# A new token order, block transposes for the first two batches and 32x32 score tiles in an attention kernel with two MoE layers

## The chip, the cores and the metric

The kernel runs on one core of one Trainium2 chip. The metric is the device time of one execution in microseconds (us). Of the kernel before, three runs took 1302.26, 1302.63 and 1302.87 us.

## The reference, cut to what matters

```python
def sm_attn(qq, kk, vv):                       # 8 batches, 8 heads, 576 tokens, head width 64
    s = scale * np.matmul(qq, kk.transpose(0, 1, 3, 2))
    a = np.exp(s - np.max(s, axis=-1, keepdims=True))
    a = a / (np.sum(a, axis=-1, keepdims=True) + 1e-09)
    return np.matmul(a, vv)
p_packed = sm_attn(p, k, v)                    # 32 packed queries a head read all tokens
x = sm_attn(q, p_packed, p_packed)             # all tokens read the 32 packed rows
...                                            # x to [4608, 512]
h = x @ w_in; x = (h - np.tanh(h)) @ w_out     # first layer, width 2048
...                                            # second layer: each token to one expert of 8, width 1024
out[mask] = gate_w[mask, None] * (np.maximum(x[mask] @ w1[e], 0.0) @ w2[e])
```

The order in which the 4608 tokens are kept on the chip is free, as long as every row of the output is written to its place.

## The kernel before, in words

**Slots.** The two layers are one row of slots, and the loop at the end of the kernel (L1047) goes through them. A slot of the first layer is a half batch (288 tokens) and one block of 128 hidden columns: `gemm1` (L719), the function h - tanh(h) in four ScalarE and four VectorE instructions (`chain`, L730), three slots later `gemm2` (L764). There are 256: slots 0 to 31 are batch 0 in plain float32, slots 32 to 255 the other batches with every operand split into a high and a low part (three products each, `mm3`, L95). The input of `gemm1` is not v: w_in is multiplied by the packed rows first (`m_pe`, L210), so that a slot multiplies softmax weights `a` by `m`. Then come 144 slots of the second layer.

**Ahead of slot 0** stand 31 more slots (-31 to -1, `NPRO` and `LEAD`) with the attention of batch 0 and the first of the weight conversions. The first of them puts the loads on the SyncE queue.

**Attention** (`attention`, L246) of batch b is hung on slots: `post` entries are loads and VectorE work, `stage(t, fn, *evs)` puts TensorE work `fn` on slot base + t and what reads its result on the next slot. All of it goes through one PSUM tile, `AT` (two banks, L68), so each stage waits until the one ahead is read out. Its steps: k transposed (head width on the partitions), scores of the packed queries (`scores1`), maximum, exponential and sum (`s1max`, `s1exp`, `s1sum`), the weights transposed (`a1t_pe`), times v (`p1_pe`), that transposed (`ppt_pe`), scores of q against the packed rows (`scores2`), softmax over 32 (`sm2a` to `sm2d`).

Two forms exist. For batches 0 and 1 (`by_pe`) k and q are loaded in 1536-byte runs and transposed on TensorE against an identity (`flip_pe`, eight calls a batch, twelve matmuls each) and copied out of `AT` (`flip_ev`). For batches 2 to 7 the loads put 32 elements (128 bytes) to a run, 32 loads a batch for k and q, and VectorE transposes 32x32 blocks (`prep`, L317, eight instructions a batch).

**Weight conversions.** w_in and w_out come as float64; 32 steps (`conv_a`, L158) turn a 512 KB piece into float32: two VectorE instructions (L161, L165), three on ScalarE (L169 to L171), one on GpSimd (L177). Four buffers take the pieces (`raw_load`, L136), loaded two steps ahead; the steps lie on slots -21 to 16. The sixteen w_out pieces are split afterwards (`conv_b`, L186).

**Batch b > 1** starts at slot 32(b-1) + 5, batch 1 at slot 0; its `m_pe` from slot 21 of its stretch of 32 on. The order inside a slot is the program's; between engines a scheduler moves instructions past each other.

Of the kernel before, what the change touches and what calls it, by code (L numbers as in the profile page):

```python
# [2 lines left out]

# [18 lines left out]
EPS = 1e-9  # L22
# [3 lines left out]
def attn_moe_moe_kernel(  # L26
# [26 lines left out]
    LAG = 3  # L53
    NWH = NF
# [54 lines left out]
    def consts2(sp):  # L109
        wg = sp.tile([128, 4, NE], F32, name="wg")  # L110
        nc.sync.dma_start(out=wg, in_=w_gate.rearrange("(c p) e -> p c e", p=128))
        md = evp.tile([32, B, 18, 2], I32, name="md", tag="rt_b")
        nc.sync.dma_start(
            out=md, in_=mod_id.bitcast(I32).rearrange("(b i k two) -> i b k two", b=B, i=32, two=2)
# [12 lines left out]
        nc.vector.tensor_copy(out=modi.rearrange("i (b k) -> i b k", b=B), in_=md[:, :, :, 0])  # L127
# [30 lines left out]
    def conv_a(key):  # L158
# [51 lines left out]
    def m_pe(b, u):  # L210
        def rhs(g, hh):
# [5 lines left out]
            lambda g, hh: AT[32 * hh:32 * hh + 32, g, 0:256],  # L217
# [4 lines left out]
    def m_ev(b, u):  # L222
        ps = AT[:, :, 0:256]
# [22 lines left out]
    def attention(ap, b):  # L246
        r = {}

        def nat_tile(shape):
            return ap.tile(shape, F32, name="nat", tag="nat", bufs=2)  # L250

        by_pe = b < 2

        def load_pair(src, nm, j):
            if by_pe:

                t = r[nm, j] = nat_tile([96, 2, 2, 6 * D])
                for g in range(2):
                    h0 = 4 * g + 2 * j
                    nc.sync.dma_start(  # L260
                        out=t[:, g], in_=src[b, h0:h0 + 2].rearrange("h (a c) d -> a h (c d)", c=6)
                    )
                return

            t = nat_tile([128, 2, 18, 32])
            for g in range(2):
                for e in range(2):
                    q0 = 64 * g + 32 * e
                    for x in range(2):
# [643 lines left out]
    with ExitStack():  # L913
# [34 lines left out]
        def place(grp, base):  # L948
# [4 lines left out]
            for t, fn in pe.items():  # L953
                at_pe(base + t, fn)
# [169 lines left out]
```

## Time and profile before

| | us |
|---|---|
| median of the three runs | 1302.63 |
| the profiled execution, its own time | 1304.62 |
| its span | 1302.9 |
| start of slot 0 (first `gemm1`) | 64.94 |
| start of slot 32 | 206.66 |
| first matmul of the second layer | 881.8 |

The span runs from the first to the last instruction of the profile; what lies around it makes the execution's own time. A stage is the stretch between two of these starts. "Busy" of an engine is the sum of its instructions in a stretch; a matmul of float32 is two rows in the trace, so `x16` is eight of them.

### The profile page before, as it was taken

The page shows a single profiled execution, that of the slowest core. Times are in us where ns is not written, and L with a number is a line of the kernel's source. Part 1 is how long each engine was busy: PE and PEld are TensorE (multiplying, and loading weights), DVE is VectorE, ACT ScalarE, POOL GpSimd, SP SyncE. Part 2 cuts the span into 40 slices and gives each one's busy share as a digit, 9 for nine tenths or more (in the row PEclk, how much of TensorE's full clock was granted, in tenths as well). Part 3 has the DMA queues.
Part 4 walks back from the last instruction along what each step waited for, and adds up shares of the span by engine and source line. Part 5 has one row for each costly group of instructions (what it writes and reads, how often), then busy time and mean ns, then how long its engine had stood idle before and what let it go on. Part 6 is the DMA issues. An engine that isn't in the chain of part 4 may idle for free.

```text
span 1302.9 us, 26482 instructions
## 1 busy us (share of the span) xinstructions
PE 1225.3 (94%) x10018; PEld 1070.6 (82%) x10019; DVE 828.0 (64%) x1931; ACT 718.4 (55%) x1848; POOL 166.7 (13%) x174
## 2 busy tenths in 40 slices
PE   4597889999999999999999999999999999999996
PEld 3365568978988988978988978989999999999995
DVE  2577699798898798898898897895212121111211
ACT  3589877777767767767777777772111111111111
POOL 1123220110111110110111112250000000000000
PEclk9998899999999999999999999999999999999998
DMA  6757535435345245245245024332221221222201
GB/s 173 199 172 203 144 90 165 101 106 146 69 114 139 64 121 147 49 123 143 48 126 144 20 96 144 95 102 69 63 84 56 67 74 64 82 65 82 66 17 35
DMA packets 192533, 132.40 MB, mean 102 GB/s; under 512 B 123280, under 2 KB 171408, under 8 KB 192400
## 3 DMA queue, kind: packets, MB, share of 16 engines
q1 hardware_dynamic: 192400, 130.65, 36.4%
q8 instruction: 80, 1.31, 0.4%
q14 instruction: 53, 0.43, 0.1%
HBM read 98.10 MB, written 32.51 MB: 100 GB/s over the span
## 4 chain that ended last, share of the span: by engine, by line
PE 70%; DVE 16%; ACT 5%; issue 4%; DMA 2%; POOL 1%; SPq 1%; DVEq 0%; ACTq 0%; POOLq 0%
PE acc L97 12%; PE acc L99 11%; PE acc L98 11%; PE h L97 9%; PE h L98 8%; PE h L99 8%; DVE gs L748 2%; DVE gs L750 2%; PE at L201 2%; PE at L294 2%; DVE th L744 2%; DVE gl L761 2%; PE acc L770 1%; DVE qq L746 1%; PE at L342 1%
## 5 line engine op out<-in xcount | busy, mean ns | idle before, releaser
L97 PE MATMUL acc<-gh,wo_hi 128*128 128x288 f32 x960 | 293.8, 308 | 6.0 <-ACT gh L759 5.1
L99 PE MATMUL acc<-gl,wo_hi 128*128 128x288 f32 x960 | 276.8, 298 | 6.3 <-DVE gl L761 3.4
L98 PE MATMUL acc<-gh,wo_lo 128*128 128x288 f32 x960 | 281.5, 295 | 0.0
L97 PEld LDWEIGHTS acc<-gh,wo_hi 128*128 128x128 f32 x960 | 179.9, 188 | 41.0 <-ACT u L740 11.4
L99 PEld LDWEIGHTS acc<-gl,wo_hi 128*128 128x128 f32 x960 | 177.1, 188 | 14.2 <-DVE gl L761 6.9
L98 PEld LDWEIGHTS acc<-gh,wo_lo 128*128 128x128 f32 x960 | 180.3, 188 | 0.7 <-issue 0.4
L99 PE MATMUL h<-xbl,w1h 128*128 128x256 f32 x576 | 162.3, 282 | 0.0
L98 PE MATMUL h<-xbh,w1l 128*128 128x256 f32 x576 | 162.1, 281 | 0.0
L97 PE MATMUL h<-xbh,w1h 128*128 128x256 f32 x576 | 161.5, 280 | 0.0
L761 POOL TENSOR_TENSOR gl<-gs,gh 128x288 fp32r<-128x288 f32 x105 | 85.6, 816 | 575.6 <-ACT gh L759 424.9
L744 DVE TENSOR_TENSOR th<-h,th 128x288 f32<-128x288 f32 x256 | 114.8, 448 | 54.9 <-ACT mk L742 51.5
L750 DVE COPY_PREDICATED gs<-mk,th 128x288 f32<-128x288 int32 x256 | 139.3, 544 | 2.8
L97 PE MATMUL h<-ah,mh 128*128 128x288 f32 x448 | 135.2, 302 | 5.7 <-DVE gs L748 5.7
L740 ACT ACTIVATE u<-h 128x288 f32<-128x288 f32 x256 | 106.4, 416 | 56.7 <-PE h L99 40.3
L862 DVE SCALAR_TENSOR_TENSOR bl<-h,bh 128x256 fp32r<-128x256 f32 x72 | 30.6, 425 | 164.0 <-ACT bh L861 163.9
L98 PE MATMUL h<-ah,ml 128*128 128x288 f32 x448 | 132.2, 295 | 0.0
L743 ACT ACTIVATE qq<-u 128x288 f32<-128x288 f32 x256 | 114.8, 449 | 30.9 <-DVE gs L748 25.0
L99 PE MATMUL h<-al,mh 128*128 128x288 f32 x448 | 131.8, 294 | 0.0
L746 DVE SCALAR_TENSOR_TENSOR qq<-qq,u 128x288 f32<-128x288 f32 x256 | 121.6, 475 | 13.4 <-ACT qq L743 10.5
L759 ACT ACTIVATE gh<-gs 128x288 fp32r<-128x288 f32 x240 | 108.0, 450 | 36.6 <-PE acc L98 35.3
L741 ACT ACTIVATE th<-h 128x288 f32<-128x288 f32 x256 | 105.0, 410 | 34.2 <-DVE gs L750 32.0
L861 ACT ACTIVATE bh<-h 128x256 fp32r<-128x256 f32 x72 | 27.6, 384 | 171.4 <-PE h L99 169.8
(145 smaller groups left out, 2462.3 us busy)
## 6 DMA issues: line engine op xcount, KB each, us to landing
ws<-w_in_v SPq DMA_DIRECT2D x56, 512.0 KB
nat<-in_v_dram SPq DMA_DIRECT2D x16, 576.0 KB
x_hi<-x2h SPq DMA_DIRECT2D x16, 576.0 KB
x_lo<-x2l SPq DMA_DIRECT2D x16, 576.0 KB
xbh<-x_hi SPq DMA_DIRECT2D x18, 512.0 KB
xbl<-x_lo SPq DMA_DIRECT2D x18, 512.0 KB
raw<-in_moe_w_in_dram SPq DMA_DIRECT2D x32, 256.0 KB
raw<-in_moe_w_out_dram SPq DMA_DIRECT2D x16, 512.0 KB
```

The source lines that it names most:

```text
L97: nc.tensor.matmul(out=ps, lhsT=ah, rhs=bh, start=first, stop=False)
L98: nc.tensor.matmul(out=ps, lhsT=al, rhs=bh, start=False, stop=False)
L99: nc.tensor.matmul(out=ps, lhsT=ah, rhs=bl, start=False, stop=last)
L740: nc.scalar.activation(out=u, in_=ps, func=ACTF.Square)
L741: nc.scalar.activation(out=th, in_=ps, func=ACTF.Tanh)
L743: nc.scalar.activation(out=qq, in_=u, func=ACTF.Exp, scale=-PK)
L744: nc.vector.tensor_tensor(out=th, in0=ps, in1=th, op=ALU.subtract)
L746: nc.vector.scalar_tensor_tensor(out=qq, in0=qq, scalar=PB, in1=u, op0=ALU.add, op1=ALU.mult)
L750: nc.vector.copy_predicated(gs, mk, th)
L759: nc.scalar.activation(out=gh, in_=gs, func=ACTF.Copy)
L761: eng.tensor_tensor(out=gl, in0=gs, in1=f32(gh), op=ALU.subtract)
L862: nc.vector.scalar_tensor_tensor(out=gl, in0=ps, scalar=0.0, in1=f32(gh), op0=ALU.max, op1=ALU.subtract)
```

## The change

**Token order.** Token t of a batch is 288a + 9i + c (a half of two, i of 32, c of 9; before 18i + 9a + c). With a and i on 64 partitions, nine tokens of a head lie behind each other: one load of k, q or v is 64 partitions x 2 heads x 2304 bytes. All batches use this form, 12 loads a batch, and v is loaded like k and q. Output rows and the modality ids follow the order.

**Transposes.** `flip_pe` and `flip_ev` are gone. `prep` transposes 32x32 blocks on VectorE, for all batches, which leaves token i on the free axis and 32 of the 64 head columns (index e) on the partitions of half a. So the products over the head width are now sums of two matmuls with 32 rows.

**Score tiles.** `scores1(g)` has 16 matmuls of 32 rows x 32 columns (before 8 of 64 x 32) and `scores2(half)` 16 (before 8). `s1exp` is one instruction of 576 elements (before two of 288). `a1t_pe` is 18 matmuls against the identity in tiles of 64 columns (before 12 transposes of 96 columns). `p1_pe` is 72 matmuls of 64 rows (before 48 of 96). `ppt_pe` has eight more matmuls, and `ppt_ev` one more copy (`ppS`).

**Start.** Batch 0's attention is no longer on slots: it is a list, written out, with six PSUM banks instead of two (`AT` and two tiles in the banks that `gemm2` takes later). Eight of the 32 conversion steps and two of the eight `m_pe` lie in that list; eight steps lie on slots 0 to 7, the rest on 8 to 20; pieces are loaded three steps ahead. Batch 1's attention starts at slot 9 (before 0), its `m_pe` at slot 25 (before 21).

```diff
-            if by_pe:
-
-                t = r[nm, j] = nat_tile([96, 2, 2, 6 * D])
...
-            t = nat_tile([128, 2, 18, 32])
...
+            t = r[nm, j] = ap.tile([128, 2, 9 * D], F32, name="nat", tag="nat", bufs=NAT)
+            for g in range(2):
+                h0 = 4 * g + 2 * j
+                nc.sync.dma_start(
+                    out=t[64 * g:64 * g + 64], in_=src[b, h0:h0 + 2].rearrange("h (a c) d -> a h (c d)", c=9)
+                )
...
+        def scores1(g):
+            ps = ps_of("s1", g)
+            for e in range(2):
+                for a in range(2):
+                    rows = slice(64 * g + 32 * a, 64 * g + 32 * a + 32)
+                    for hh in range(4):
+                        nc.tensor.matmul(
+                            out=ps[32 * hh:32 * hh + 32, a, 0:HW],
+                            lhsT=r["pT"][rows, hh, e, :],
+                            rhs=r["kT", hh // 2][rows, hh % 2, :, e, :],
+                            start=(e == 0), stop=(e == 1), tile_position=(64 * g + 32 * a, 32 * hh),
+                        )
...
-            av = r["a1", g].rearrange("p c i m -> p c (i m)")
-            for c in range(6):
-                nc.tensor.transpose(AT[0:96, c // 3, 128 * (c % 3):128 * (c % 3) + 128], av[:, c], ident)
...
+        def a1t_pe(n):
+            ps = ps_of("a1t", n)
+            for c in range(6 * n, min(6 * n + 6, 9)):
                 for g in range(2):
...
+                        lhsT=r["a1", g][:, c].rearrange("p a i -> p (a i)"), rhs=ident,
                         start=True, stop=True, tile_position=(0, 64 * g),
...
+        def p1_pe():
+            ps = ps_of("p1", 0)
+            for c in range(9):
                 for hh in range(4):
...
+                    for g in range(2):
+                        rows = slice(64 * g, 64 * g + 64)
                         nc.tensor.matmul(
...
+                            start=(c == 0), stop=(c == 8), tile_position=(64 * g, 32 * hh),
                         )
...
         def ppt_pe():
...
+            for e in range(2):
+                for q0 in range(0, 128, 32):
+                    nc.tensor.matmul(
+                        out=ps[q0:q0 + 32, 0, 128 + 128 * e:256 + 128 * e],
+                        lhsT=r["pps"][:, q0 // 64, 32 * e:32 * e + 32], rhs=ident,
+                        start=True, stop=True, tile_position=(0, q0),
+                    )
...
         def scores2(half):
...
+            ps = ps_of("s2", half)
+            for e in range(2):
+                for hh in range(4):
+                    for g in range(2):
+                        q0 = 64 * g + 32 * half
+                        nc.tensor.matmul(
+                            out=ps[32 * hh:32 * hh + 32, g, 0:HW],
+                            lhsT=r["ppS"][q0:q0 + 32, e, hh, :],
+                            rhs=r["qT", hh // 2][q0:q0 + 32, hh % 2, :, e, :],
+                            start=(e == 0), stop=(e == 1), tile_position=(q0, 32 * hh),
+                        )
...
+        A.load_pair(k, "k", 0)
+        A.load_p()
+        A.load_pair(k, "k", 1)
+        A.load_pair(q, "q", 0)
+        raw_load(ck[0])
+        raw_load(ck[1])
+        consts()
+        run(A.prep_p, lambda: A.prep("k", 0))
+        A.load_pair(v, "v", 0)
+        run(lambda: A.prep("k", 1))
+        A.load_pair(v, "v", 1)
+        A.scores1(0)
+        A.scores1(1)
+        run(lambda: A.prep("q", 0))
...
+        run(lambda: A.s1max(0), lambda: A.s1exp(0), lambda: A.s1max(1), lambda: A.s1exp(1))
+        A.a1t_pe(0)
+        run(lambda: A.s1sum(0), lambda: A.s1sum(1), lambda: conv_step(0))
+        A.a1t_ev(0)
+        A.a1t_pe(1)
+        run(lambda: conv_step(1))
...
+        A.scores2(0)
+        A.scores2(1)
+        m_pe(0, 0, X[1])
+        run(lambda: conv_step(3), lambda: A.sm2a(0), lambda: A.sm2b(0), lambda: m_ev(0, 0, X[1]))
...
-            place(attention(ap, b), 2 * NF * (b - 1) + (0 if b == 1 else 5))
+            place(attention(ap, b, lambda *key: AT).stages(), 2 * NF * (b - 1) + (9 if b == 1 else 5))
```

TensorE, from the first instruction to the first `gemm1`, before (`at` is the PSUM tile, L294 the flips, L725 `gemm1`):

```order
L294 MATMUL at<-ident,nat 64x96 x48
L342 MATMUL at<-T,pT 32x288 x16
L294 MATMUL at<-ident,nat 64x96 x48
L385 MATMUL at<-ident,a_210 96x128 x6
L385 MATMUL at<-ident,a_240 96x128 x6
L396 MATMUL at<-nat,a1T 32x64 x48
L414 MATMUL at<-ident,pps 64x128 x2
L201 MATMUL at<-T,ppT 32x288 x8
L201 MATMUL at<-wv,ppT 32x256 x8
L201 MATMUL at<-T,ppT 32x288 x8
L201 MATMUL at<-wv,ppT 32x256 x16
L725 MATMUL h<-a2w,m_w 128x288 x2
```

The same place in the changed kernel, from `p1_pe` on (L352; `x_105` and `x_106` are the two further PSUM tiles, L396 `scores2`, L203 `m_pe`, L673 `gemm1`):

```order
L352 MATMUL x_105<-nat,a1T 32x64 x72
L371 MATMUL x_106<-ident,pps 64x128 x2
L377 MATMUL x_106<-ident,pps 32x128 x8
L396 MATMUL at<-T,ppS 32x288 x16
L396 MATMUL x_105<-T,ppS 32x288 x16
L203 MATMUL x_106<-wv,ppT 32x256 x8
L203 MATMUL at<-wv,ppT 32x256 x8
L673 MATMUL h<-a2w,m_w 128x288 x5
```

The 96 flips are gone, and the stages that stood behind each other in `at` now lie in three tiles. Two `m_pe` stand ahead of the first `gemm1`, before three.

VectorE in the changed kernel, in the softmax of the first half of batch 0, from the maximum (L412) to the transpose that `gemm1` waits for (L438); L163 and L167 are conversion steps:

```order
L412 TENSOR_REDUCE m_401<-s_398 128x18
L414 TENSOR_TENSOR s_398<-s_398,m_401 128x576
L163 TENSOR_SCALAR raw_219<-raw_219 128x512
L167 SCALAR_TENSOR_TENSOR raw_219<-raw_219 128x512
L427 TENSOR_REDUCE m_427<-s_398 128x18
L163 TENSOR_SCALAR raw_237<-raw_237 128x512
L429 TENSOR_SCALAR m_427<-m_427 128x18
L167 SCALAR_TENSOR_TENSOR raw_237<-raw_237 128x512
L431 RECIPROCAL m_427<-m_427 128x18
L433 TENSOR_TENSOR s_398<-s_398,m_427 128x576
L163 TENSOR_SCALAR raw_335<-raw_335 128x512
L438 STREAM_TRANSPOSE a2w<-s_398 128x576
```

Three conversion steps, the fourth to sixth of the 32, stand in that chain with five of their six instructions. The second half's softmax comes behind it; before, its first instructions stood between those of the first half.

## Rows read from the trace of the kernel before

**Rows 1.** The page: span, and busy time, share and instructions of each engine over the whole span.

```profile
span 1302.9 us, 26482 instructions
PE 1225.3 (94%) x10018; PEld 1070.6 (82%) x10019; DVE 828.0 (64%) x1931; ACT 718.4 (55%) x1848; POOL 166.7 (13%) x174
```

**Rows 2.** Busy time by stage: stretch in us, its length, then busy us of each engine (instructions in brackets), the granted clock of TensorE, the mean share of the DMA engines and GB/s. The stretches are: ahead of slot 0; slots 0 to 16; slots 17 to 31; slots 32 to 255; the second layer.

```profile
0.00:64.94 64.94, 34.60 (x417) 22.79 (x418) 24.58 (x64) 28.68 (x57) 10.09 (x16) 1.00 0.72 185
64.94:154.37 89.43, 75.96 (x573) 53.32 (x573) 65.06 (x135) 76.69 (x169) 26.76 (x23) 0.90 0.68 190
154.37:206.66 52.29, 48.06 (x378) 36.10 (x377) 50.77 (x115) 40.27 (x107) 8.15 (x8) 1.00 0.37 109
206.66:881.80 675.14, 656.29 (x6019) 585.87 (x6018) 599.55 (x1414) 501.25 (x1347) 119.30 (x125) 1.00 0.40 105
881.80:1302.90 421.10, 410.37 (x2639) 372.50 (x2638) 88.09 (x206) 71.48 (x173) 2.43 (x3) 0.99 0.20 64
```

**Rows 3.** TensorE's waits ahead of slot 0 (0 to 64.9 us): for whom, us in total, how often, the longest.

```profile
PE at L294 <- ACT T L305: 5.3, 3, 3.8
PE at L294 <- DMA nat<-in_k_dram: 4.6, 2, 4.2
PE at L294 <- DVE T L313: 4.4, 3, 1.5
PE at L201 <- DVE s L436: 3.2, 2, 2.0
```

**Rows 4.** Groups of instructions ahead of slot 0 (0 to 64.94 us): line, engine, operation, out<-in, shapes, count, busy us and mean ns of one, idle time before them.

```profile
L294 PE MATMUL at<-ident,nat 96*64 96x96 f32 x192 | 18.0, 372 | 16.8 <-ACT T L305 5.3 <-DMA nat<-in_k_dram 4.6 <-DVE T L313 4.4
L165 DVE SCALAR_TENSOR_TENSOR raw<-raw 128x512 int32<-128x512 int32 x10 | 6.9, 687 | 0.3
L169 ACT ACTIVATE raw<-raw 128x512 int32<-128x512 f32 x9 | 6.0, 668 | 6.7 <-DVE raw L165 6.6
L161 DVE TENSOR_SCALAR raw<-raw 128x512 int32<-128x512 int32 x10 | 4.7, 468 | 11.8 <-DMA raw<-in_moe_w_in_dram 11.8
L396 PE MATMUL at<-nat,a1T 96*32 96x64 f32 x96 | 2.8, 311 | 0.9 <-ACT a1T L389 0.9
L369 ACT ACTIVATE a<-at,nm 128x288 f32<-128x288 f32 x4 | 2.0, 497 | 5.3 <-DVE nm L356 5.3
L389 ACT ACTIVATE a1T<-at 96x768 f32<-96x768 f32 x2 | 1.6, 807 | 2.9 <-PE at L385 2.9
L351 DVE TENSOR_REDUCE mx<-at 128x2 f32<-128x576 f32 x2 | 1.5, 758 | 9.8 <-PE at L342 9.8
L414 PE MATMUL at<-ident,pps 128*64 128x128 f32 x4 | 0.7, 445 | 0.6 <-ACT pps L408 0.6
```

**Rows 5.** The timeline at some places of the first 66 us: start, us, engine, line, what, count, idle time before it and what ended it.

```profile
4.17 0.55 PE L294 MATMUL at<-ident,nat 96*64 96x96 f32 x2 [4.17 <-DMA nat<-in_k_dram]
19.99 2.15 PE L342 MATMUL at<-T,pT 64*32 64x288 f32 x16 [0.75 <-ACT T L305]
55.28 0.85 DVE L436 STREAM_TRANSPOSE s<-at 128x288 f32<-128x288 f32 x2 [3.17 <-PE at L201]
64.12 0.77 DVE L467 STREAM_TRANSPOSE a2w<-s 128x576 f32<-128x576 f32 x1
64.94 2.29 PE L725 MATMUL h<-a2w,m_w 128*128 128x288 f32 x4 [0.49 <-DVE a2w L467]
```

**Rows 6.** Slots 0 to 31 (64.94 to 206.66 us): groups as in Rows 4, then TensorE's longest wait in that stretch.

```profile
L169 ACT ACTIVATE raw<-raw 128x512 int32<-128x512 f32 x23 | 15.8, 688 | 4.8 <-DVE raw L165 3.6 <-POOL wv L177 0.6
L294 PE MATMUL at<-ident,nat 96*64 96x96 f32 x192 | 12.4, 293 | 3.4 <-ACT m_w L226 2.1 <-DVE T L313 1.2
L315 ACT ACTIVATE T<-at 128x288 f32<-128x288 f32 x4 | 2.7, 686 | 1.0 <-PE at L294 1.0
L313 DVE COPY T<-at 128x288 f32<-128x288 f32 x4 | 2.7, 674 | 1.0 <-ACT T L315 1.0
L305 ACT ACTIVATE T<-at 128x576 f32<-128x576 f32 x4 | 2.6, 648 | 0.8 <-PE at L294 0.8
PE h L725 <- DVE gs L748: 8.0, 4, 3.9
```

**Rows 7.** TensorE in batch 4's attention (timeline, columns as in Rows 5): `scores1`, one `a1t_pe`, `p1_pe`, `ppt_pe`, one `scores2`.

```profile
417.91 1.17 PE L342 MATMUL at<-T,pT 64*32 64x288 f32 x16
429.98 0.82 PE L385 MATMUL at<-ident,a 128*96 128x128 f32 x6
440.93 1.55 PE L396 MATMUL at<-nat,a1T 96*32 96x64 f32 x96
448.42 0.44 PE L414 MATMUL at<-ident,pps 128*64 128x128 f32 x4
453.75 0.71 PE L201 MATMUL at<-T,ppT 64*32 64x288 f32 x16
```

**Rows 8.** TensorE's largest waits in slots 32 to 255 (206.66 to 881.8 us).

```profile
PE h L97 <- DVE gs L748: 5.7, 11, 1.3
PE acc L97 <- ACT gh L759: 3.1, 6, 0.5
PE at L201 <- DVE rt_t L555: 3.1, 6, 0.5
```

**Rows 9.** VectorE's 32x32 block transposes of k and q over the whole span, columns as in Rows 4.

```profile
L320 DVE STREAM_TRANSPOSE T<-nat 128x576 f32<-128x576 f32 x48 | 36.8, 766 | 0.0
```

More of the change, by code (lines that the diff above doesn't have):

```diff
@@ L2 @@
 from inspect import isgenerator
+from types import SimpleNamespace
 import concourse.bass as bass
@@ L333, in scores1 @@
         def scores1(g):
-            rows = slice(64 * g, 64 * g + 64)
-            for half in range(2):
-                for hh in range(4):
-                    kk = r["kT", hh // 2][rows, hh % 2]
-                    if by_pe:
-                        kk = kk[:, 9 * half:9 * half + 9, :].rearrange("p r i -> p (r i)")
-                    else:
-                        kk = kk.rearrange("p (m c) i -> p m c i", m=3)[:, :, 3 * half:3 * half + 3, :]
-                    nc.tensor.matmul(
-                        out=AT[32 * hh:32 * hh + 32, half, 0:HW],
-                        lhsT=r["pT"][rows, hh, :],
-                        rhs=kk,
-                        start=True, stop=True, tile_position=(64 * g, 32 * hh),
-                    )
+            ps = ps_of("s1", g)
@@ L705, in other_half @@
                 )
-            rows = out[bass.ds(b * S, S), :].rearrange("(i r) d -> r i d", r=18)[9 * half + 3 * t:9 * half + 3 * t + 3]
+            rows = out[bass.ds(b * S + half * HW, HW), :].rearrange("(i c) d -> c i d", c=9)[3 * t:3 * t + 3]
             o = ox.tile([96, 512], F32, name="oo")
@@ L977, in at_cv @@
             cv_ev.setdefault(n, []).append(fn)
-        NPRO = 24
-        LEAD = 7
-        place(attention(ap, 0), -NPRO)
+        NPC = 8
+        cslot = {}
+        for i in range(len(ck) + 1):
+            if i < NPC:
+                m = -1
+            elif i < 2 * NPC:
+                m = i - NPC
+            else:
+                m = 8 + (i - 2 * NPC) * 3 // 4
+            if m >= 0:
+                at_cv(m, lambda i=i: conv_step(i))
+            if i < len(ck):
+                cslot[ck[i]] = m
@@ new lines, in attn_moe_moe_kernel, with run @@
+        for f in range(NWH // 2):
+            at_cv(NWH + 1 + f * 11 // 7, lambda f=f: conv_b((1, f)))
+        def run(*fns):
+            for _ in seq(fns):
+                pass
+        ps0 = tc.alloc_tile_pool(name="ps0", bufs=1, space=PSUM)
+        X = [ps0.tile([128, 2, 512], F32, name=f"x{c}") for c in range(2)]
+        PS0 = {
+            ("s1", 0): AT, ("s1", 1): X[0], ("a1t", 0): X[1], ("a1t", 1): AT, ("p1", 0): X[0], ("ppt", 0): X[1],
+            ("s2", 0): AT, ("s2", 1): X[0],
+        }
@@ L1046, in attn_moe_moe_kernel @@
         total = len(slots)
-        for n in range(-NPRO - LEAD, total + LAG + 2):
-            if n == NF + 1:
+        for n in range(total + LAG + 2):
+            if n == NF + 5:
                 early.release()
```

328 lines of the change are left out of this document (128 added, 200 removed).

## The prediction

> **What bounds the kernel now.** I read the busy shares first, then the busy time by stage, then the waits and the single rows of each stage. TensorE is busy 94% of the span [rows 1], but the stages differ [rows 2]. In the second layer (881.8 us on) it has 410 of 421 us of work; the change leaves that stage alone. In slots 32 to 255 it has 656 of 675 us; VectorE has 600. Ahead of slot 0 no engine is the bound: TensorE is busy 34.6 of 64.9 us, ScalarE 28.7, VectorE 24.6. There the reader is to see a chain: flips wait for ScalarE's copies, for VectorE's copies and for k [rows 3], because everything goes through one PSUM tile. In slots 0 to 31 (141.7 us) three engines share the load: TensorE 124.0 us, ScalarE 117.0, VectorE 115.8 (two rows of that view added) [rows 2].
>
> So there are three places to look at: how much earlier slot 0 starts, whether slots 0 to 31 keep their length, and what the longer attention costs where TensorE is full.
>
> **The start.** Slot 0 starts at 64.94 and waits last for the transposed softmax of half 0 [rows 5]. I follow the new list from row to row. The first flip got its first k load at 4.17 [rows 5]. The queue now holds k and p (1.3 MB by shape) before anything else; at the 185 GB/s of this stretch [rows 2] that is 7.1 us, so k is there at 8 (estimate; 7 to 10). Two block transposes of 0.77 [rows 9]: 9.6. `scores1(0)`, 2.15 at the durations of this stretch [rows 5]: 11.8. The maximum, then two block transposes of q that stand ahead of the negation, the other maximum, small steps: 0.76 + 1.53 + 0.76 + 0.5 [rows 4, 9]: 15.3. Two exponentials, each less than two of 0.50 and more than one, say 0.9 [rows 4]: 17.1. On ScalarE five of the first six conversion instructions stand ahead of the copy of the transposed weights, 5 x 0.67 and 0.81 [rows 4]: 21.2; TensorE's transposes run beside that. `p1_pe`, 2.8 before [rows 4], now nine rounds for twelve but 144 rows for 96, so 2.1 to 4.2, and it waits for the second copy: 25. Two copies, `ppt_pe` (0.7 and two more rounds), two more copies [rows 4]: 28.5. `scores2(0)`, now two rounds, 2.15: 30.7. The softmax of half 0 took 9.6 from its first transpose to the end of its last, 55.28 to 64.89 [rows 5], with conversion steps and half 1 between its instructions; now other conversion steps stand there and half 1 doesn't, so 9: 39.7. The sixth conversion piece, which VectorE reads ahead of the last transpose, is the 6.8th MB of the queue: 37 us at 185 GB/s, 26 if the engines, busy at 0.72 [rows 2], were filled. That hides behind the chain, just. Slot 0 at 39.5: **-25.4 us** (35 to 46: -30 to -19).
>
> **Slots 0 to 31.** What moves in or out, by engine. TensorE loses batch 1's flips, 12.4 us [rows 6], and gains about 2.5 (one `m_pe` more, the longer attention below): 114. ScalarE had run nine conversions' first instruction before slot 0 [rows 4], now five: 4 x 3 x 0.67 = +8.0; it loses eight copies, 2.7 + 2.6 [rows 6], and about 1.0 of exponentials: 119. VectorE had begun ten, now six: 4 x (0.47 + 0.69) = +4.6 [rows 4]; it gains eight block transposes, +6.1 [rows 9], loses four copies, -2.7 [rows 6], and gains the part of half 1's softmax that now falls behind slot 0, about 2.4: 126. The sum over the three is 357 before and 359 now, only shifted from TensorE to VectorE. So I keep the length and add a little, because VectorE was already busy 50.8 of 52.3 us in slots 17 to 31 [rows 2] and four conversions now end there: **+3 us** (-9 to +11).
>
> **Slots 32 to 255**, six batches of attention, all on a full TensorE. `scores1` took 1.17 for two rounds of 288 columns, `scores2` 0.71 for one [rows 7], so a round is 0.46 (1.6 ns a column) and starting a group 0.25. `scores1` keeps two rounds: 0. `scores2` gets a second: 2 x 0.46 = +0.92. `a1t_pe`: nine rounds of 128 columns, 1.84, with two starts 2.34, for 2 x 0.82 [rows 7]: +0.70. `ppt_pe`: two rounds of 128: +0.41. `p1_pe`: twelve rounds in 1.30 and a start before [rows 7], now nine: -0.32; if it is the 16 ns an instruction (1.55 / 96) that set its time, 144 of them make 2.3: +0.78. The Trainium skill, "TensorE: Matmul & The Clock Gate", part 1, has a rule that speaks against many small matmuls: starts are never closer than some 25 ns, by which `p1_pe` would be 3.6 us, +2.1, and the kernel, by an estimate from that page, near 1298. The trace disagrees with it: 96 rows in 1.55 us are 16 ns apart [rows 7]. No row shows tiles of 32 rows; I take eight at a time, as the 64-row tiles of `scores2` ran, and keep four at a time as the other end (a rival below). Sum +1.7 a batch (to 2.8), +10 in six (to 17). Against it stands TensorE's idle time here, 18.9 us [rows 2]; the named waits are for VectorE and ScalarE being late [rows 8], mostly behind `scores2`. The new matmuls stand ahead of them, so VectorE gets that time and part of the waits closes; I give back 6. ScalarE's shorter exponentials and the larger DMA runs are costed at nothing: none of these waits is for a DMA, and ScalarE is busy only 501 of 675. Net **+4 us** (-2 to +17).
>
> **Sum.** -25.4 + 3 + 4 = -18.4. The profiled execution took 1304.62, 2.0 above the median 1302.63, so 1286.2 in its terms and **1284** as a median.
>
> **Rivals.**
> *The gain is given back in slots 0 to 31.* VectorE at 126 us is the fullest engine, slots 17 to 31 were full of it, and four conversions with three splits (some 7 us) go there; pieces must also come at 190 GB/s or more, with the engines at 0.68 [rows 2]. TensorE waited 8.0 us for VectorE here [rows 6], and its granted clock was 0.90 in slots 0 to 16 [rows 2], part of that stretch at the lower of 1.2 and 2.4 GHz; more waiting could bring more of it. For it: these rows. Against: the total load does not grow. Price +10 over the forecast: 1294.
> *`p1_pe` and its like are bound by instructions.* At the 16 ns of rows 7, `p1_pe` costs +0.78 and not -0.32, and the same rate on the other added rows adds about as much again in the six batches with nothing left to absorb it: +6, 1290. The rule of the Trainium skill weighed above, in "TensorE: Matmul & The Clock Gate", lies beyond this case in the same direction.
> *Slower: tiles of 32 rows run four at a time.* Place: `scores1`, `scores2`, `p1_pe` in the six full batches. `scores1` and `scores2` go to four rounds: 2 x 0.92 + 2 x 1.38; `p1_pe` to 18 rounds of 0.108: +0.64; with +0.70 and +0.41 that is 6.35 a batch, 38 in six, of which the idle time takes 12 at most: +26. At the start two calls double, and `p1_pe`: +6; batch 1: +5. Net -25.4 + 3 + 6 + 5 + 26 = +15: 1317. It decides from about 4.5 us more a batch. For it: no row has such tiles. Against: two groups of 64 rows ran together (0.71 for 16 matmul rows against 1.17 with one group) [rows 7]. The Trainium skill, "TensorEngine Tiling (Array Packing)", Key Properties, says that tiles work independently, and lists 16 of them for 32x32; that speaks for eight at a time, and the trace agrees for tiles of 64 rows.
> *Better.* Slot 0 at 36, slots 0 to 31 shorter by 8 since TensorE waits less for one PSUM tile, the waits of rows 8 gone: 1270.
>
> **Numbers.** Forecast 0.56; given back 0.18; instructions 0.10; better 0.08; slower 0.08. Range 1269 to 1299: below it half of the better case, above it the slower case and a quarter of the given-back one. A difference under 0.2% (2.6 us) can't be told from no change. Faster: the forecast, instructions, better and 0.11 of the given-back case, 0.85; the same: 0.06 of that case; slower: 0.01 of it and the slower case, 0.09.
>
> **What would show it.** First `gemm1` at 36 to 43 us; first high/low product of slot 32 at 178 to 194; slots 32 to 255 in 673 to 685 us; `scores2` near 1.2 us for 32 matmul rows, `scores1` too, `a1t_pe` 2.3 in both, `p1_pe` 1.2. VectorE and not TensorE the fullest engine in slots 0 to 31. Wrong if `scores1` takes near 2.1 us, if slot 0 starts after 46, or if slots 0 to 31 take more than 155 us.

## The result, and the profile after

The changed kernel took **1312.26 us** (median; four runs, 1311.21 to 1313.25), the kernel before 1302.45 in the runs beside it: 1.008 of it, 95% interval 1.0062 to 1.0099. It is slower by 0.8%; the forecast was 1284. The profiled execution took 1311.34, 6.7 more than the profiled one of before (1304.62); the shares of the stages below are shares of these 6.7, not of the 9.8 between the medians.

The page of the changed kernel: span, then busy us, share and instructions of each engine.

```profile
span 1309.6 us, 27913 instructions
PE 1232.9 (94%) x10850; PEld 1064.0 (81%) x10851; DVE 840.4 (64%) x1939; ACT 705.7 (54%) x1808; POOL 167.5 (13%) x174
```

Busy time by stage, columns as in [rows 2]: ahead of slot 0; slots 0 to 31; slots 32 to 255; second layer.

```profile
0.00:42.00 42.00, 19.44 (x361) 10.95 (x362) 20.81 (x52) 14.97 (x29) 6.80 (x12) 0.85 0.75 188
42.00:195.60 153.60, 126.60 (x910) 82.72 (x909) 125.98 (x269) 122.14 (x279) 38.16 (x36) 0.91 0.62 173
195.60:888.90 693.30, 676.49 (x6947) 597.76 (x6946) 605.48 (x1415) 497.34 (x1330) 120.07 (x125) 1.00 0.35 104
888.90:1309.60 420.70, 410.40 (x2640) 372.53 (x2638) 88.12 (x206) 71.27 (x173) 2.45 (x3) 0.99 0.21 64
```

Against [rows 2] the start is 22.9 us shorter (forecast 25.4), slots 0 to 31 are 11.9 longer (forecast 3), slots 32 to 255 18.2 longer (forecast 4), and the second layer is 0.4 shorter: +6.7 in the span. The start came within its range. Both other stages failed.

**Slots 0 to 31.** The same view in three pieces, slots 0 to 15, 16 to 23, 24 to 31; the changed kernel first, the kernel before second.

```profile
42.00:112.44 70.44, 58.15 (x294) 34.84 (x293) 59.83 (x125) 56.12 (x127) 18.18 (x17) 0.94 0.76 209
112.44:164.36 51.92, 41.72 (x424) 27.34 (x423) 36.06 (x74) 44.13 (x98) 13.98 (x13) 0.84 0.60 161
164.36:195.62 31.26, 26.76 (x197) 20.56 (x195) 30.11 (x72) 21.91 (x55) 5.99 (x6) 0.95 0.36 109
```

```profile
64.94:146.48 81.54, 68.85 (x540) 49.05 (x540) 60.53 (x128) 71.14 (x156) 25.71 (x22) 0.93 0.68 194
146.48:179.99 33.51, 30.23 (x216) 20.82 (x217) 29.40 (x64) 25.83 (x66) 4.08 (x4) 0.91 0.42 101
179.99:206.66 26.67, 24.93 (x194) 19.55 (x193) 25.90 (x60) 20.00 (x53) 5.11 (x5) 1.00 0.39 128
```

Slots 0 to 15 gained another 11.1 us: at slot 16 the change was 34.0 us ahead. Slots 16 to 23 lost 18.4 of it and slots 24 to 31 another 4.6. Before, slots 17 to 31 had no conversion and little attention left; now the last conversions, most of batch 1's attention and the split products of `gemm2` (from slot 16 on its operands are split, in both kernels, and those of `gemm1` not; the description above, which has all of slots 0 to 31 in plain float32, is wrong there) meet there. Of the 18.4 us in slots 16 to 23, 11.5 are more busy time of TensorE (41.7 for 30.2; part of it is the lower clock) and 6.9 more idle time. No engine is full there: ScalarE is busy 0.85 of it, and TensorE idles 10.2 us. Over all of slots 0 to 31 it is the other way round: of the 11.9 us, 2.6 are busy time of TensorE and 9.3 idle time.

TensorE's largest waits in slots 0 to 31 of the changed kernel:

```profile
PE h L673 <- DVE gs L696: 9.5, 8, 2.8
PE at L203 <- POOL wv L179: 7.3, 11, 1.5
PE acc L718 <- POOL wv L179: 3.4, 4, 1.4
```

The wait for `gs` was there before (8.0, [rows 6]). New is the one for the last conversion instruction: 10.7 us, before 1.3, at `gemm2` alone; by its size, 9.4 us more, it would fill the 9.3 of idle time, but the experiments below do not bear out that the stretch is longer by it. Two of TensorE's groups in that stretch of the changed kernel, then `m_pe` in the kernel before:

```profile
L673 PE MATMUL h<-a2w,m_w 128*128 128x288 f32 x128 | 44.9, 474 | 9.7 <-DVE gs L696 9.5
L203 PE MATMUL at<-wv,ppT 64*32 64x256 f32 x98 | 9.6, 452 | 7.5 <-POOL wv L179 7.3 <-ACT a L313 0.2
```

```profile
L201 PE MATMUL at<-wv,ppT 64*32 64x256 f32 x80 | 3.3, 390 | 0.2 <-DVE s L436 0.2
```

`m_pe` of batch 0 stands there six times, not five, and now each comes in two halves of eight rows, as its two weight pieces are done: 9.6 us of TensorE for 3.3 (8.3 for 3.1 by the distance to the next start). How close the slots now stand behind the conversions, GpSimd's and TensorE's rows show: the last instruction of the second piece of `m_pe` 6 and 7, then the first `gemm1` of slots 20 and 22; below them the last w_in piece before and slot 22 before.

```profile
131.63 1.36 POOL L179 TENSOR_TENSOR wv<-raw 128x512 f32<-128x512 f32 x1 [2.49 <-ACT raw L172]
149.03 1.12 POOL L179 TENSOR_TENSOR wv<-raw 128x512 f32<-128x512 f32 x1 [1.27 <-ACT raw L172]
136.57 2.12 PE L673 MATMUL h<-a2w,m_w 128*128 128x288 f32 x4
152.84 2.29 PE L673 MATMUL h<-a2w,m_w 128*128 128x288 f32 x4
```

```profile
138.31 2.66 POOL L177 TENSOR_TENSOR wv<-raw 128x512 f32<-128x512 f32 x1 [6.02 <-ACT raw L170]
169.85 1.13 PE L725 MATMUL h<-a2w,m_w 128*128 128x288 f32 x4
```

The last w_in piece was done at 141.0 before and is done at 150.1 now, though slot 0 starts 23 us earlier: the row of conversions did not move with slot 0. Slot 22 started 28.9 us after its piece before, and 2.7 after it now. The `gemm1` rows at 2.12 and 2.29 us instead of 1.13 are at the lower of the clock's two levels (granted 0.51 and 0.50).

**Slots 32 to 255.** Four batches, slots 64 to 191, of the changed kernel and of the kernel before (columns as in [rows 2]):

```profile
298.06:699.18 401.12, 393.72 (x4194) 345.44 (x4193) 352.92 (x836) 284.87 (x762) 58.64 (x64) 1.00 0.35 103
```

```profile
305.95:694.53 388.58, 380.17 (x3587) 337.52 (x3585) 348.39 (x836) 288.09 (x774) 58.26 (x64) 1.00 0.42 106
```

+12.5 us, 3.1 a batch: TensorE's work grew by 3.4 a batch and its idle time fell by 0.25. Batch 4's attention, to be held against [rows 7]; each step with the row behind it, since what a step costs is the distance to the next start (a row's own time overlaps the next row's).

```profile
425.41 1.53 PE L330 MATMUL at<-ident,a 128*64 128x128 f32 x24 [0.36 <-ACT a L313]
426.87 0.40 PE L99 MATMUL acc<-gh,wo_hi 128*128 128x288 f32 x1
431.83 0.88 PE L330 MATMUL at<-ident,a 128*64 128x128 f32 x12
432.64 0.40 PE L99 MATMUL acc<-gh,wo_hi 128*128 128x288 f32 x1
437.60 1.67 PE L352 MATMUL at<-nat,a1T 64*32 64x64 f32 x144
439.20 0.40 PE L99 MATMUL acc<-gh,wo_hi 128*128 128x288 f32 x1
445.62 0.44 PE L371 MATMUL at<-ident,pps 128*64 128x128 f32 x4
445.99 0.65 PE L377 MATMUL at<-ident,pps 128*32 128x128 f32 x16
446.56 0.40 PE L99 MATMUL acc<-gh,wo_hi 128*128 128x288 f32 x1
457.61 1.20 PE L396 MATMUL at<-T,ppS 32*32 32x288 f32 x32
```

```profile
430.56 0.38 PE L97 MATMUL acc<-gh,wo_hi 128*128 128x288 f32 x1
442.41 0.40 PE L97 MATMUL acc<-gh,wo_hi 128*128 128x288 f32 x1
448.79 0.40 PE L97 MATMUL acc<-gh,wo_hi 128*128 128x288 f32 x1
```

By starts `a1t_pe` takes 1.46 + 0.81 = 2.27; before, 430.56 - 429.98 = 0.58, and the second piece alike. `p1_pe` takes 1.60, before 442.41 - 440.93 = 1.48; `ppt_pe` 0.94, before 448.79 - 448.42 = 0.37. The six batches agree on each of these within 0.02 us.

### The profile page after: what moved, and what is told of

Same layout as the page of the kernel before. It is cut to its first block, busy times and chain, and to the rows that moved or that the text cites. A ratio compares the mean times of both kernels' runs of the same rounds, so it can differ in the third digit from the quotient of the medians.

```text
span 1309.6 us, 27913 instructions
## 1 busy us (share of the span) xinstructions
PE 1232.9 (94%) x10850; PEld 1064.0 (81%) x10851; DVE 840.4 (64%) x1939; ACT 705.7 (54%) x1808; POOL 167.5 (13%) x174
## 4 chain that ended last, share of the span: by engine, by line
PE 62%; DVE 16%; issue 7%; ACT 4%; DMA 2%; POOL 1%; SPq 0%; POOLq 0%; DVEq 0%; ACTq 0%
PE acc L99 12%; PE acc L101 11%; PE acc L100 11%; PE h L99 8%; PE h L101 8%; PE h L100 8%; DVE gs L696 3%; DVE gs L698 2%; DVE th L692 2%; DVE qq L694 2%; PE at L203 2%; DVE gl L709 1%; PE at L330 1%; ACT mk L690 1%; DVE s L407 1%
## 5 line engine op out<-in xcount | busy, mean ns | idle before, releaser
L101 PE MATMUL acc<-gl,wo_hi 128*128 128x288 f32 x960 | 282.1, 299 | 2.9 <-POOL gl L709 1.3
L694 DVE SCALAR_TENSOR_TENSOR qq<-qq,u 128x288 f32<-128x288 f32 x256 | 128.1, 500 | 6.8 <-ACT qq L691 3.3
L691 ACT ACTIVATE qq<-u 128x288 f32<-128x288 f32 x256 | 114.5, 447 | 25.0 <-DVE gs L696 18.9
L689 ACT ACTIVATE th<-h 128x288 f32<-128x288 f32 x256 | 104.7, 409 | 31.9 <-DVE gs L698 28.5
```

What stands on the lines that cost most here:

```text
L101: nc.tensor.matmul(out=ps, lhsT=ah, rhs=bl, start=False, stop=last)
L689: nc.scalar.activation(out=th, in_=ps, func=ACTF.Tanh)
L691: nc.scalar.activation(out=qq, in_=u, func=ACTF.Exp, scale=-PK)
L694: nc.vector.scalar_tensor_tensor(out=qq, in0=qq, scalar=PB, in1=u, op0=ALU.add, op1=ALU.mult)
```

## Experiments

Times are medians; "before" is the kernel before in the same job (1301.7 to 1303.4). "Slots 0 to 31" is from the first `gemm1` to the first product of slot 32 in the profile; 153.6 us in the changed kernel. Such a stretch comes from one execution; the same instructions took 141.7 and 139.6 us in two of them (before and e2), so a difference of 2 us in it shows nothing by itself. Medians of different jobs are compared as they stand; before's own differ by 1.6.

**e1: the steady attention, score tiles undone.**

```diff
+        wide = b >= 2
+            if wide:   # scores1; scores2 alike; k, q, p loaded 32 elements to a run
+                        nc.tensor.matmul(
+                            out=ps[32 * hh:32 * hh + 32, a, 0:HW], lhsT=pT[rows, 32 * hh:32 * hh + 32],
+                            rhs=kk[:, 288 * a:288 * a + 288], start=True, stop=True, tile_position=(64 * g, 32 * hh),
+                        )
-            for e in range(2):
+            for e in range(0 if wide else 2):   # ppt_pe's added matmuls
```

> The changed kernel, with one part undone in batches 2 to 7: k, q and p are loaded as before (32 elements to a run), so scores1 and scores2 are 8 matmuls each of 64 rows x 32 columns again, and ppt_pe and ppt_ev lose what they had gained. Token order, start list, batches 0 and 1, a1t_pe and p1_pe stay. Theory A (the added matmul rows cost their own time on a full TensorE, 2.6 us a batch, and nothing is given back): of these rows, scores1 0.17, scores2 0.97 and ppt_pe 0.64 a batch go, 1.8 x 6 = 10.7: 1301.5 (1299.5 to 1303.5); slots 32 to 255 fall from 693 to about 682.5. Theory B (slots 32 to 255 are longer because VectorE and ScalarE come late, not by TensorE's own rows): 1309 or more.

1307.86 (1.0037 of before, 1.0023 to 1.0051): 4.4 less than the change, between the two forecasts. Slots 32 to 255 took 688.4, 4.9 less than the change and not 10.7. In slots 64 to 191:

```profile
297.82:693.74 395.92, 388.18 (x3874) 341.48 (x3873) 352.93 (x838) 285.62 (x758) 58.58 (x64) 1.00 0.43 107
```

TensorE's work fell by 1.4 a batch, the time by 1.3. In these four batches that is theory A at three quarters of its price (1.8). In the waits of e1's slots 32 to 255 a reader of `AT` stands where there were 2.3 us:

```profile
PE at L203 <- DVE ml L234: 7.5, 6, 1.2
```

A wait of 1.47 us ahead of slot 216 cost more: the clock went to its lower level there (0.57 over the 8 us), and 2.7 us beyond the wait were lost against the change. No run undid the new `a1t_pe`; its price rests on the rows above.

```profile
769.00:777.00 8.00, 6.59 (x29) 5.35 (x29) 6.61 (x14) 3.45 (x10) 1.62 (x2) 0.57 0.21 66
770.41 0.61 PE L99 MATMUL h<-ah,mh 128*128 128x288 f32 x1 [1.47 <-DVE gs L747]
```

**e2: does idle time give back?**

```diff
+            for _ in range(2 if b > 1 else 1):   # kernel before, scores2
                 tiled(
```

> The kernel before, with scores2 of batches 2 to 7 issued twice (the same values again). It measures whether TensorE's idle time gives back added matmul time. One scores2 is 0.71 us, the repeated eight matmuls 0.46 to 0.71; twelve of them 5.5 to 8.5 us. Theory A (nothing is given back): 1308 to 1311. The forecast's step (the idle time of 18.9 us takes 6 of it): 1302.5 to 1305.

1304.15, +0.9 (1.0013, 1.0003 to 1.0022). The total misleads: slots 0 to 31, untouched, came out 2.1 us shorter in the profiled run. In slots 32 to 255:

```profile
204.13:881.20 677.07, 661.88 (x6211) 589.69 (x6210) 596.95 (x1414) 500.18 (x1347) 119.09 (x125) 1.00 0.40 105
```

TensorE's work is 5.6 more than before, the time 1.9. The stretches of 32 slots with the attention of batches 2 to 6 each grew by 0.72 to 0.83 us for 0.9 of added matmuls; the one with batch 7's fell by 1.3, as a wait of 0.8 for `gs` went, and the last one by 0.6. So a fifth is given back batch by batch, and the rest at single waits. Neither theory holds whole, and that the median fell into the range of the forecast's step was luck.

**e3: m_pe a slot later.** `cslot[0, u, 1] + 1` becomes `+ 2`.

> The changed kernel, with batch 0's m_pe from the third on placed two slots behind the conversion of its second piece, not one. In slots 0 to 31 TensorE waits 7.3 us for GpSimd's last conversion step at m_pe and 3.4 us at gemm2 (1.3 before). Theory C (slots 0 to 31 are longer because TensorE, in order, stands at m_pe until the conversion is done): the 7 us go, about 1305 (1303 to 1308). Theory D (ScalarE is full in that stretch, and the waits only show it): 1311 to 1313, the waits move to other places.

1314.01; slots 0 to 31 153.5. C's forecast fell, and D's was missed by a little: the waits for GpSimd were 9.8 and 2.8. But most `m_pe` stood within 1.4 us of their times in the change (two came 2 to 4 us later), so the edit hardly tested C.

**e4: less work on ScalarE.**

```diff
-        nc.scalar.activation(out=hi.bitcast(F32), in_=hi, func=ACTF.Sign)
-        nc.scalar.activation(out=lo.bitcast(F32), in_=lo.bitcast(F32), func=ACTF.Abs)
+        nc.scalar.activation(out=hi.bitcast(F32), in_=hi, func=ACTF.Sign, scale=-1.0)
```

> The changed kernel, with two of ScalarE's three instructions a conversion step left: Abs goes, and Sign takes scale -1 (the low word is the negative of the magnitude wherever a weight is below 2, so the product is the same for these weights). That takes 0.57 us of issue a step off ScalarE, 24 steps behind slot 0: 13.7 us. Theory D (ScalarE is full in slots 10 to 25 and sets their length): 8 to 12 us less, 1300 to 1304. Theory C (the place of m_pe): at most 3 us less, 1309 or more.

1319.09, **slower** by 6.8. Slots 0 to 31:

```profile
42.76:205.03 162.27, 133.44 (x909) 88.52 (x909) 126.70 (x269) 109.30 (x253) 39.31 (x36) 0.83 0.61 163
```

ScalarE had 12.8 us less to do, and D fell. TensorE waited 15.1 us for converted weights at `m_pe`, and with the granted clock at 0.83, not 0.91, the same matmuls took 6.8 us more.

**e5, e9, e10: batch 1's attention at slot 2, 6, 13 (change: 9).** `place(..., 9 if b == 1 ...)` becomes 2, 6, 13; in e5 and e9 loads that fall ahead of slot 0 go to slot 0.

> The changed kernel, with batch 1's attention seven slots earlier (base 2, not 9; loads that would stand ahead of slot 0 go to slot 0). In slots 8 to 16 the change gained 14.0 us, in slots 16 to 32 it lost 23.0. Theory E (batch 1's attention now meets the conversions and the split products of slots 16 to 24; load was displaced, not removed): slots 16 to 24 fall from 51.9 to 45 or less, slots 8 to 16 rise by less, in all 3 to 6 us less: 1306 to 1309. Theory F (the conversions behind slot 0 set the pace of slots 0 to 24, whatever stands beside them): within 1.5 us of 1312.

> The changed kernel, with batch 1's attention at slot 6 (in e5_b1_early 2, in the change 9; its first loads go to slot 0, six slots ahead of the matmuls that need them). In e5_b1_early slots 16 to 32 were 10.6 us shorter, but slots 0 to 8 12.8 us longer, where TensorE stood 3.7 us for p and k. Theory E (attention in slots 16 to 24 costs because it meets conversions and splits there): with the loads in time slots 16 to 32 keep 4 to 8 us of that gain and slots 0 to 16 rise by 2 to 6: 1307 to 1312. If the length of slots 0 to 16 rises by more than slots 16 to 32 fall, the load is only moved between slots that have no room: above 1313.

> The changed kernel, with batch 1's attention four slots later (slot 13). The conversions end at slot 20; most of the attention's matmuls then stand behind them, its softmax on VectorE in slots 25 to 32. Theory E (meeting the conversions costs): slots 16 to 24 shorter by 4 or more. Theory G (VectorE, 0.96 busy in slots 24 to 32, sets that end): slots 24 to 32 longer by as much or more as the softmax moves there: 1312 to 1318 in all.

e5 1318.29, e9 1315.77, e10 1310.49; slots 0 to 31 159.3, 156.7, 149.0. Slots 16 to 31 fell to 72.6 in e5 (83.2 in the change), slots 0 to 15 rose to 86.8 from 70.4: both E's forecast and F's were missed. In e9 and e10 slots 16 to 23 took 55.9 and 54.7, more than the 51.9 of the change: E fell, the attention's place alone isn't what makes them long. In e10 slots 24 to 31 took 30.0, 1.3 less, so G's forecast for them fell too; the gain is in slots 0 to 15 (64.3), and slots 32 to 63 took 104.7 for 102.5. Moved earlier, the attention costs more than it frees; moved later, a little less.

**e6: the splits of the first eight w_out pieces later.** `at_cv(NWH + 1 + f * 11 // 7, ...)` becomes `at_cv(31 + f, ...)`.

> The changed kernel, with the high/low splits of the first eight w_out pieces at slots 31 to 38, not 17 to 28 (their first use is at slot 35). Theory G (VectorE, 0.96 busy in slots 24 to 32, and ScalarE set the end of the stretch): 8 x 0.6 us go from VectorE and 8 x 0.57 from ScalarE, and slots 20 to 32 are 4 to 6 us shorter, with room for them behind slot 32: 1306 to 1308. Rival (the waits come from the order on TensorE, VectorE's share only shows it): 1310.5 or more.

1309.83, between the two forecasts. Slots 20 to 31 took 55.5 (59.1 in the change): 3.5 less where G had 4 to 6, and 2.6 of it in slots 20 to 23, not in slots 24 to 31, where VectorE is full. Slots 0 to 15 took 1.3 more, and slots 32 to 63, where the splits now stand, 2.0 more (104.4): there was no room behind slot 32.

**e7: no conversion behind slot 0.**

```diff
+        if skip:   # steps 8 to 31
+            nc.gpsimd.tensor_scalar(out=v, in0=lo, scalar1=0.0, scalar2=0.01, op0=ALU.is_equal, op1=ALU.mult)
```

> The changed kernel, with the conversions behind slot 0 left out: 24 of the 32 steps are one GpSimd instruction that writes constants, in place of two VectorE, three ScalarE and one GpSimd instruction; the loads stay. The weights are then not the reference's, and only slots 0 to 31 are read. Theory F (the conversions set the pace): slots 0 to 31 fall from 153.6 to 130 or less, near TensorE's own work. Theory E (displaced attention, splits): 140 or more.

Slots 0 to 31, then slots 16 to 23 and 24 to 31 of them:

```profile
43.22:186.30 143.08, 121.57 (x908) 81.87 (x909) 102.38 (x223) 82.06 (x207) 60.48 (x36) 0.93 0.71 190
105.63:149.57 43.94, 36.83 (x401) 26.27 (x399) 20.40 (x44) 22.88 (x57) 18.71 (x11) 0.96 0.54 142
149.57:186.30 36.73, 27.80 (x220) 19.63 (x221) 36.59 (x82) 24.73 (x62) 6.85 (x6) 0.95 0.55 161
```

143.1, as E had it; F's 130 was not reached. In this one execution leaving out the conversions gains 10.5 us, 5.0 of busy time of TensorE and 5.5 of idle time. Without the work of conversion on VectorE and ScalarE the stretch is still as long as before (141.7 with all of it), because work was moved: slots 16 to 23 take 43.9, before 33.5, with 36.8 us of TensorE's work, before 30.2, and VectorE and ScalarE half idle; slots 24 to 31 take 36.7, with VectorE full. And the last w_in piece, now one GpSimd instruction, still came at 143.5, with slot 22 2.4 us behind it: a slot that starts just behind its piece need not be held up by the work of converting it.

**e12, e14, e16: the conversions' place, their splits, their order.**

```diff
-                m = 8 + (i - 2 * NPC) * 3 // 4
+                m = 8 + (i - 2 * NPC) // 2          # e12
-                yield from conv_b(ck[i - 1])
+                yield from conv_b(ck[i - 2])        # e14, behind conv_a; loads two ahead
-            ck += [(0, u, 0), (0, u, 1), (1, 2 * u), (1, 2 * u + 1)]
+            ck += [(0, u, 0), (0, u, 1)]            # e16
+            if u > 4: ck += [(1, 2 * u - 2), (1, 2 * u - 1)]
```

> The changed kernel, with the last sixteen conversion steps two to a slot on slots 8 to 16 (in the change four on three slots, 8 to 20), and with them batch 0's last m_pe. Theory H (the steps come late because of their place in the program, and TensorE stands 10.7 us for them): the waits for GpSimd fall by 6 or more, slots 16 to 24 by 8 or more, 1302 to 1307. Theory I (the engines have no room: ScalarE is busy 0.8 to 0.9 in slots 8 to 24, and a step earlier pushes a chain later): slots 8 to 16 rise by about what slots 16 to 24 fall: 1309 to 1314.

> The changed kernel, with the split of a w_out piece two conversion steps behind its conversion, as before, not one (from step 16 on; a piece is then loaded two steps ahead, not three). From 75 to 157 us VectorE, in order, stands 15.0 us at the split's subtraction until ScalarE has copied the product; before it stood 4.0 us there. Theory J (that stand holds up the chain and the next steps, and so TensorE): VectorE's wait falls to 7 us or less, slots 16 to 24 are 4 to 8 us shorter, 1304 to 1308. Rival (VectorE's stand is idle time that ScalarE's load sets, or the pieces then come late): slots 16 to 24 within 2 us of 51.9, 1310 or more.

> The changed kernel, with the last sixteen pieces converted in the order in which the slots need them: w_in of m_pe 5, 6 and 7 two steps earlier (steps 19, 23 and 27, not 21, 25 and 29), w_out behind. In the changed kernel slot 18 starts 3.8 us after step 21 is done, slot 20 3.6 after step 25, slot 22 2.7 after step 29; before, slot 22 started 28.8 us after its last piece. Theory K (slots 18 to 22 hang on the conversion stream, which starts no earlier than before and goes on at some 4.5 us a step): slot 22 comes 5 to 9 us earlier, and the kernel takes 1304 to 1308. Rival (the stream only keeps step with slots that something else holds up): slot 22 within 2 us of 152.8, 1310 or more.

1318.04, 1313.87, 1317.44; slots 0 to 31 158.2, 156.2, 158.0. In e12 the steps came no earlier in time (step 29 done at 148.5, 150.1 in the change): H fell, and I with it, since slots 16 to 23 did not shorten (55.1). In e14 VectorE's stand fell to 5.9 us, and TensorE's wait for GpSimd rose to 17.3 and slots 16 to 23 to 57.1: J fell, and of the rival's two marks one. In e16 the pieces of slot 18 were done 16 us ahead of it, and it still began at 120.7 (120.3 in the change), waiting for VectorE; slot 20 came 5.4 earlier and slot 24 2.3 later. Slot 22, K's mark, came at 151.6, 1.2 earlier and not 5 to 9: K fell, and the rival's forecast held.

**e8, e11, e13, e15, e17, e18: edits together.** e8 is e1 with e5 and e6; e11 is e1 with e6. e13, e15 and e17 are e11 with e10 and with e12, e14 or e16. e18 is e17 with `m_pe` of batches 2 to 7 at slot 22, not 21.

> The changed kernel, with the 64-row score tiles of e1_wide_scores and the late splits of e6_splits_late. Each alone: 1307.9 and 1309.8 against 1312.3. If the two stretches are apart, as theories A and G have it: 4.4 + 2.4 less, 1305.5 (1303.5 to 1307.5).

> The changed kernel, with the 64-row score tiles, the late splits, batch 1's attention at slot 13 and the pieces in the order of need. With e13_four_together (the steps earlier in place of the order) 1305.3. With theory K 1297 to 1302, at or below the kernel before; without, 1304 to 1308.

> The kernel of e17_wide_splits_13_need, with m_pe of batches 2 to 7 one slot later (from slot 22 of a stretch of 32, not 21). In e1_wide_scores and e17_wide_splits_13_need the second m_pe of each batch stands 1.25 us in AT until VectorE, behind the softmax of the second half, has read the first out (0.4 in the changed kernel); that is why e1_wide_scores gave 1.3 us a batch and not 1.8. If so, the wait goes and 6 x 0.8 to 1.2 us with it: 1296 to 1299 against 1302.9, faster than the kernel before. If the wait only moves to another reader of AT: 1301 to 1305.

e8 1310.82, e11 1306.41, e13 1305.34, e15 1308.19, e17 **1302.88** (0.9996 of before, 0.9983 to 1.0009), e18 1308.17. e11 came within 1 us of the sum of its parts. e8 and e15 were slower than either of their forecasts (1296 to 1301 or 1306 to 1309; 1298 to 1302 or 1303 to 1307), e13 came where theory I put it (1303 to 1307), e17 stands between its two, and e18 is above both of its own. e17 equals the kernel before; no version beat it. e16's order, 5 us worse alone, was 2.5 better than e12's with the attention at slot 13. Slots 0 to 31 of e17:

```profile
43.21:187.59 144.38, 123.53 (x915) 82.93 (x913) 125.91 (x260) 118.96 (x274) 38.06 (x36) 0.91 0.66 174
```

They are 9.2 us shorter than in the change, although TensorE stands 14.0 us there for GpSimd's last conversion instruction (10.7 in the change). So this wait does not measure what the conversions cost. By pieces, in us:

| | slots 0 to 15 | 16 to 31 | 32 to 63 | 64 to 255 |
|---|---|---|---|---|
| before | 81.5 | 60.2 | 99.3 | 575.8 |
| change | 70.4 | 83.2 | 102.5 | 590.8 |
| e1, score tiles | 70.5 | 82.8 | 101.4 | 587.1 |
| e6, splits late | 71.7 | 79.7 | 104.4 | 590.4 |
| e10, attention at 13 | 64.3 | 84.7 | 104.7 | 590.5 |
| e17 | 61.0 | 83.4 | 107.1 | 587.7 |
| e18 | 61.1 | 83.3 | 106.4 | 591.6 |

e17's gain lies in slots 0 to 15; slots 16 to 31 are as long as in the change, and slots 32 to 63 give 5.7 back against e1. Load was moved once more, not taken away. (e17's profiled execution was 2.4 us above its median.)

In e18 the wait for `ml` went (7.5 us in e17), and another for VectorE took part of its place: the first two rows of TensorE's waits in its slots 32 to 255.

```profile
PE acc L101 <- DVE gl L760: 6.0, 6, 1.0
PE h L99 <- DVE gs L747: 4.0, 10, 1.0
```

In all, TensorE's idle time there fell by 2.2 us (21.0 to 18.8). But its work rose by 5.4, and the rows of `m_pe` are all of that: at the new slot 17 of the 52 `m_pe` were issued in two pieces with other matmuls between (7 in e17), and a piece costs nearly what a whole one does. One of them, with the row behind each piece:

```profile
383.18 0.62 PE L203 MATMUL at<-ws,ppT 64*32 64x256 f32 x2
383.73 0.40 PE L99 MATMUL h<-ah,mh 128*128 128x288 f32 x1
384.71 0.66 PE L203 MATMUL at<-ws,ppT 64*32 64x256 f32 x14
385.30 0.40 PE L99 MATMUL acc<-gh,wo_hi 128*128 128x288 f32 x1
```

Two rows take 0.55 us, fourteen 0.59, and a whole `m_pe` of sixteen 0.59. That is what the two halves of batch 0's `m_pe` pay in the change, too. Whether e18's expectation, 0.8 to 1.2 us a batch, would have come with whole `m_pe` isn't shown.

## Why the prediction was wrong

**The start was right.** By the trace `p1_pe` began at 22.7, `scores2(0)` at 30.1 and was done at 32.3 (forecast 30.7), `gemm1` began at 42.0 (39.5; named interval 36 to 43). Of the 25 us that the forecast was off, the start is 2.5, slots 0 to 31 are 9 and slots 32 to 255 are 14.

**Slots 0 to 31: the step "the sum over the three is 357 before and 359 now, so I keep the length" failed.** VectorE's 126 was right (125.98), ScalarE's 119 nearly (122.1), TensorE's 114 not: 126.6. The flips went (12.4), but `m_pe`, once more and in halves, cost 5.1 more, which is more than the 2.5 that I had for it and the longer attention together, and more of the stretch ran at the lower clock (0.91, before 0.94). An equal sum was also no ground for an equal length: slots 0 to 15, which had room, became shorter, and slots 16 to 31, which had little, got the load. The first rival named this stage and price (+13; measured +11.9) and its reasons in part: VectorE full in slots 24 to 31 (30.1 of 31.3) and the clock. Its condition on the loads was not what came: in slots 0 to 31 no row of VectorE's waits is for a piece. I gave it 0.18.

What I overlooked is that slot 0 moved 23 us ahead and the conversions did not. They began at 16 us, before at 12, and the last w_in piece came at 150, before at 141, with slot 22 due at some 144 by my own forecast (39.5 and the 105 us from slot 0 to slot 22 of before); and the new order of the pieces puts that w_in pair at steps 28 and 29, before at 26 and 27. That this is what lengthens the stretch is argued, not shown. For it: TensorE's waits for these pieces, and the 10.5 us of e7. Against it: e7's last piece came at 143.5 with next to nothing to compute, e16's order did not bring slot 22 forward, and e17 is shorter with longer waits. The cause inside this stage stays open. Place, order, splits, ScalarE's load and `m_pe`'s place were each changed alone, and none of the five kernels was faster than the change: e4, e12 and e16 were slower by 5.2 to 6.8 us, e3 and e14 by 1.6 to 1.8, which is not clear of the noise. Each edit also moved other instructions on the in-order engines and, with them, the clock, so none is a clean subtraction. Shown is that slots 16 to 31 hold more work than before (TensorE is busy 68.5 us there, before 55.2, part of it at the lower clock), that three edits together take 9.2 us off slots 0 to 31, and that slots 32 to 63 give 5.7 of that back (against e1).

**Slots 32 to 255: two terms failed.** The first is the sum of the steps, +1.7 a batch. For `a1t_pe` I had +0.70. Its new time was right (forecast 2.34, by starts 2.27), its old one wrong: I took 0.82 each from rows whose end overlaps the next matmul, where 0.58 is the distance to the next start. The cost is +1.11. `p1_pe`, off by as much, is +0.12 and not -0.32: nine rounds for twelve saved nothing. `ppt_pe` is +0.57 and not +0.41, `scores2` about +1.0 (+0.92), `scores1` near 0. Together +2.8 a batch for 1.7, 17 us in six, the bound that I kept for the range. TensorE's busy time grew by 20.2; the other 3 us are not assigned to a step. The second is the 6 us that I gave back from idle time: it fell from 18.9 to 16.8, by 2. e2 shows the same for eight added matmuls alone, a fifth given back batch by batch. The reason, as I read it and no run isolates it: VectorE is late at its own place, and matmuls ahead of it push VectorE's inputs later as well.

**The rivals.** Tiles of 32 rows ran eight at a time: `scores1` 1.20 for 32 rows, 1.17 for 16 of twice the height [rows 7]; the slower case did not come about by its mechanism. The case of instructions bound by number came about in part: `p1_pe` with 144 rows took 1.60 us, more than its rounds but 11 ns a row and not 16. The Trainium skill, "TensorE: Matmul & The Clock Gate", part 1, has starts never closer than 25 ns, by which it would be 3.6, an estimate; the trace disagrees, with 11 ns. The miss is that of the first rival's stage together with one in slots 32 to 255 that is more than twice the second rival's price; the range had been cut as if only one could come.

## What to carry to other kernels

When a stage starts earlier, ask of each stream that feeds it (here, converted weights) whether it moves too, and of the slots behind whether they have room for what no longer stands in front. Price a step on a full TensorE by the distance to the next start, in the old kernel as in the new. Count into how many pieces a group of small matmuls falls: a piece can cost what the whole does. Give nothing back from idle time unless the engine that is waited for gets its inputs no later. Where three engines share a stretch, add up loads by small pieces of it, not over the whole. And when an edit shortens a stretch, look at the next one for the load.

## What the hardware showed beyond expectation

- Small matmuls have no fixed price a row: 96 rows of 96 x 32 by 64 columns took 1.48 us from start to next start (15 ns), 144 rows of 64 x 32 took 1.60 (11 ns).
- `m_pe` (64 x 32 tiles by 256 columns) costs by pieces: 2 rows 0.55 us to the next start, 8 rows 0.57, 14 rows 0.59, 16 rows 0.59 (change and e18; 8 rows at the lower clock 1.01).
- A single wait of 1.47 us on a TensorE otherwise full was followed by the clock's lower level and cost 2.7 us beyond itself (e1). In slots 0 to 31, the kernel with 12.8 us less work on ScalarE ran at a mean granted clock of 0.83 for 0.91 and took 8.7 us longer, 6.8 of them busy time of TensorE (e4).
